# Scores as three half-height products per head, even and odd heads on the two halves of TensorE's rows

## The chip, the core and the metric

The kernel runs on one core of a Trainium2 chip. Its engines work side by side, each through its own list of instructions in the order of the program: TensorE (PE: matrix products; PEld: the loads of its stationary operand), VectorE (DVE), ScalarE (ACT), GpSimd (POOL) and SyncE (SP, which issues most of the DMAs). TensorE writes to PSUM, which has eight banks of 2 KB in each of 128 partitions. The metric is the device time of one launch in microseconds; less is better.

## What is computed

Three blocks follow each other. Attention with a window of 128 positions for 4 sequences of 576 tokens and 8 heads of 64; a mixture of 4 experts (512 to 1024 to 512, weighted by given probabilities); and a soft mixture of 8 experts with 4 slots each. The change touches the first alone:

```python
B, H, S, D = q.shape                  # 4, 8, 576, 64
scores = scale * np.matmul(q, k.transpose(0, 1, 3, 2))
bias = slopes[:, None, None] * (-np.abs(rel).astype(np.float32))[None, :, :]
mask = (rel >= 0) & (rel < window)    # window 128
scores = np.where(mask, scores + bias[None], -1000000000.0)
attn = np.exp(scores - np.max(scores, axis=-1, keepdims=True))
attn = attn / (np.sum(attn, axis=-1, keepdims=True) + 1e-09)
out = np.matmul(attn, v)
```

## The kernel before, in words

The 2304 tokens are 18 tiles of 128. A tile needs the keys of itself and of the tile before it, two key blocks (one for the first tile of a launch or of a sequence that begins on a tile's edge). Numbers in float32 are split into a high and a low float16 part, so that a product of two of them is three float16 products: high by high, high by low, low by high.

**Scores.** `sp_qk_hi` and `sp_qk_lo` (lines 336 to 343) split q and k of a tile; for each head the 64 high columns stand beside the 64 low ones. `tr_q` and `tr_k` turn this over (a DMA transpose, TensorE for the first two tiles), so that a head has its high part in rows 0 to 63 and its low part in rows 64 to 127. One product over 128 rows then gives high by high plus low by low (line 393). For the mixed terms `swap_q` (lines 375 to 378) makes a second copy of q with the halves exchanged, two copies on VectorE, and line 398 adds the second product. A head and a key block take 2 products of 128 by 128 by 128. Line 396 adds the mask of tiles in which a sequence ends. `qk` does this for two heads (a head pair), whose scores lie in one PSUM bank; tags S0 and S1, one bank each, take turns from pair to pair.

**Softmax and values.** `soft` adds the bias and takes the maximum (line 409, VectorE), the exponential (414) and the float16 parts (419 on ScalarE, 420 on GpSimd), then transposes them. `pv` (line 440) multiplies with v into one of two banks, X0 or X1, for four heads each; `xn` normalises (lines 449 to 451).

**Order.** `att_step` emits one step per tile and head pair, 72 in all; products with v trail by up to three steps. The first mixture's products are emitted between the steps: lines 300 and 310 in float32 for tiles 0 and 1, 242 and 261 for tiles 2 to 7 with expert 0, then units of 256 hidden columns (first layer: 742, later 727 from seven sums; second layer: 829). Line 193, with 192, splits the weights. A scheduler that works with its own timeline then sets each engine's final order; the text's order is not the program's. TensorE takes its list strictly in that order. From tile 8 on, the first layer holds the bank X1 too (its tile C).

Of the kernel before, what the change touches and what calls it, by code (L numbers as in the profile page):

```python
# [20 lines left out]
def kernel(  # L21
# [47 lines left out]
    def nm(s):  # L69
        uid[0] += 1  # L70
        return f"{s}_{uid[0]}"
# [262 lines left out]
            raw[nme, i] = t  # L334

    def sp_qk_hi(nme, i):
        t = at([P, H, 2, D], F16, nme + "s", 1)
        nc.scalar.activation(out=t[:, :, 0], in_=raw[nme, i], func=AF.Copy)
        (qqs if nme == "q" else kks)[i] = t

    def sp_qk_lo(nme, i, eng):
        t = (qqs if nme == "q" else kks)[i]
        return eng.tensor_tensor(out=t[:, :, 1], in0=raw[nme, i], in1=t[:, :, 0], op=ALU.subtract).ins

    def sp_v_hi(i):
        vvs[i] = vbuf[i % 4]
# [16 lines left out]
        nc.scalar.activation(out=dst[:, hb:nb], in_=pt[:, hb:nb], func=AF.Copy)  # L363

    def tr_k(i, pe=False):
        t = at([P, H, P], F16, "kT", 3)
        trans(t, kks[i].rearrange("p h a d -> p (h a d)"), H, pe)
        kT[i] = t

    def tr_q(i, pe=False):  # L370
        t = at([P, 2, H, P], F16, "qT", 2)
        trans(t[:, 0], qqs[i].rearrange("p h a d -> p (h a d)"), H, pe)
        qT[i] = t

    def swap_q(i):
        t = qT[i]
        nc.vector.tensor_copy(t[0:D, 1], t[D:P, 0])
        nc.vector.tensor_copy(t[D:P, 1], t[0:D, 0])  # L378

    def kbs(i):  # L380
        return [1] if i in first else [0, 1]

    fixes = {(0, 0): P, (0, 1): P // 2, (1, 0): P // 2}

    def qk(i, hp):
        st = ps.tile([P, 2, 2 * P], F32, tag=f"S{hp % 2}", name=nm("s"), bufs=1)
        fix = 0 if i in split else (1 if (i - 1) in split else None)
        for hl in range(2):
            h = 2 * hp + hl
            for kb in kbs(i):  # L390
                o = st[:, hl, kb * P:(kb + 1) * P]
                mv = kT[i - 1 + kb][:, h]
                nc.tensor.matmul(o, lhsT=qT[i][:, 0, h], rhs=mv, start=True, stop=False)  # L393
                fx = fixes.get((fix, kb))
                if fx:
                    nc.tensor.matmul(o[:, 0:fx], lhsT=(fixa if fix == 0 else ones1), rhs=negs[:, 0:fx],
                                     start=False, stop=False)
                nc.tensor.matmul(o, lhsT=qT[i][:, 1, h], rhs=mv, start=False, stop=True)  # L398
        return st

    def soft(i, hp, st):
        kb0 = kbs(i)[0]
        if hp == 0:
            nmx[i] = at([P, H], F32, "nmx")
        c0, w = kb0 * P, (2 - kb0) * P
        et = at([P, 2, 2 * P], F32, "e", 3)
        for hl in range(2):
            h = 2 * hp + hl
            mx = nc.vector.tensor_tensor_reduce(out=et[:, hl, c0:], in0=st[:, hl, c0:], in1=bias[:, h, c0:],  # L409
                                                op0=ALU.add, op1=ALU.min, scale=-0.125, scalar=3.0e38,  # L410
                                                accum_out=nmx[i][:, h:h + 1])
        for hl in range(2):
            h = 2 * hp + hl
            nc.scalar.activation(out=et[:, hl, c0:], in_=et[:, hl, c0:], func=AF.Exp, scale=-1.0,  # L414
                                 bias=nmx[i][:, h:h + 1])
        e2 = at([P, 2, 2, 2 * P], F16, "e2", 3)
        if kb0:
            e2 = e2.rearrange("p a b c -> p (a b c)")[:, 0:4 * P].rearrange("p (a b c) -> p a b c", a=2, b=2)
        nc.scalar.activation(out=e2[:, :, 0], in_=et[:, :, c0:], func=AF.Copy)  # L419
        nc.gpsimd.tensor_tensor(out=e2[:, :, 1], in0=et[:, :, c0:], in1=e2[:, :, 0], op=ALU.subtract)  # L420
        nb = 4 * w // P
        eTt = at([P, 8, P], F16, "eT", 5)
        trans(eTt[:, 0:nb], e2.rearrange("p a b c -> p (a b c)"), nb, i < 2)
        eT[i, hp] = eTt
        return mx.ins

    def pv(i, hp):
        if hp % 2 == 0:
            xps[i, hp // 2] = ps1.tile([P, 512], F32, tag="X0" if i >= SG[1][0] + SG[1][1] else f"X{hp // 2}", name=nm("x"))[:, 0:4 * (D + 1)].rearrange(
                "p (h d) -> p h d", h=4)  # L430
        nk = len(kbs(i))
        kb0 = kbs(i)[0]
        t = eT.pop((i, hp))
        for hl in range(2):
            h = 2 * hp + hl
            o = xps[i, hp // 2][:, h % 4]
            for kb in kbs(i):
                for ea, va in ((0, 0), (0, 1), (1, 0)):
                    w = D + 1 - va
                    nc.tensor.matmul(o[:, 0:w], lhsT=t[:, (hl * 2 + ea) * nk + kb - kb0],  # L440
                                     rhs=vvs[i - 1 + kb][:, h, va, 0:w],
                                     start=(kb == kb0 and ea == 0 and va == 0), stop=(kb == 1 and ea == 1))
# [68 lines left out]
        build_bias(scr, range(6, H))  # L511
    tr_q(0, True)
    tr_k(0, True)
    swap_q(0)
    sp_v_hi(0)
    sp_v_lo(0)
    LAG = 3
# [37 lines left out]
    def att_step(n, work=None):  # L555
# [18 lines left out]
        if n < NS:  # L574
            if hp < 3 and i + 2 < NT:
                ld(i + 2, "qkv"[hp])
            if i + 1 < NT:
# [6 lines left out]
                    sp_qk_lo("k", i + 1, nc.gpsimd)  # L584
                elif hp == 2:
                    tr_k(i + 1, i + 1 < PE_T)
                    swap_q(i + 1)
                    sp_v_hi(i + 1)
                else:
                    sp_v_lo(i + 1)  # L590
# [723 lines left out]
```

## Time and profile before

| what | us |
|---|---|
| three timed runs | 931.27, 931.63, 937.0 |
| their median | 931.63 |
| the profiled execution: its own time | 936.76 |
| its span, first to last instruction | 935.0 |

The profile is of one execution, 5.1 us above the median of the three. Busy time is the time in which an engine had an instruction under way. TensorE's products are pipelined: the length of one says how long it takes from start to (modelled) end, and the next may start long before that, so the pace is read from the distance of starts. A timeline row that says x6 is six instructions in one row.

### The profile page before, as it was taken

What the parts mean: (1) busy time and instruction counts of PE and PEld (TensorE: products, weight loads), DVE (VectorE), ACT (ScalarE), POOL (GpSimd) and SP (SyncE); (2) the same over time, 40 slices, a digit from 0 to 9 for tenths busy, and PEclk for the clock granted to TensorE, in tenths of its full rate; (3) what the DMA queues carried; (4) which work ended last, traced back from release to release, by engine and by line L of the source; (5) the groups of instructions that cost most, each with busy time, mean ns of one, the idle gap of its engine ahead of it and who ended that gap; (6) DMA issues with size and microseconds to landing.
All of it is one profiled execution on the core that took longest, in us unless ns stands there. A gap on an engine that the chain in (4) does not pass through costs nothing.

```text
span 935.0 us, 16158 instructions
## 1 busy us (share of the span) xinstructions
PE 885.7 (95%) x6302; PEld 509.6 (55%) x6302; DVE 535.4 (57%) x1225; ACT 389.4 (42%) x806; POOL 183.4 (20%) x177
## 2 busy tenths in 40 slices
PE   5779799899999999999999999999999899999797
PEld 3747567554544454545555555555556566666432
DVE  5965755535645445548866775687554465445422
ACT  5965555534634343434445443445232233222222
POOL 4544454400221221300102010150021100000000
PEclk9889899999999999999999999999999999999799
DMA  9699998937785564344545645497674855437896
GB/s 262 118 184 199 207 208 145 166 56 199 186 172 132 143 136 113 68 107 141 126 141 152 180 125 159 142 344 226 181 167 163 185 208 192 161 132 252 303 377 233
DMA packets 252813, 165.80 MB, mean 177 GB/s; under 512 B 191120, under 2 KB 221872, under 8 KB 252736
## 3 DMA queue, kind: packets, MB, share of 16 engines
q1 hardware_dynamic: 249616, 153.65, 62.9%
q0 software_dynamic: 3120, 11.11, 4.0%
q8 instruction: 49, 0.80, 0.3%
q14 instruction: 28, 0.23, 0.1%
HBM read 104.44 MB, written 27.79 MB: 141 GB/s over the span
## 4 chain that ended last, share of the span: by engine, by line
PE 75%; DVE 6%; DMA 6%; issue 6%; ACT 2%; POOL 1%; SPq 0%; ACTq 0%; POOLq 0%; DVEq 0%
PE l L829 31%; PE l L742 12%; PE A L727 9%; PE C L727 4%; PE l L242 2%; DMA xtb<-xsb 2%; PE B L727 2%; DVE w L193 2%; PE hp L1246 2%; PE x L440 2%; PE so_ps L1264 2%; PE l L261 2%; PE l2f L310 1%; PE fp L1277 1%; DMA XA<-xs 1%
## 5 line engine op out<-in xcount | busy, mean ns | idle before, releaser
L829 PE MATMUL l<-w,HA 128*128 128x512 f16 x1536 | 366.5, 381 | 0.3 <-DVE acc L271 0.3
L829 PEld LDWEIGHTS <-HA 128*128 128x128 f16 x1536 | 148.1, 98 | 157.6 <-issue 5.0
L727 PEld LDWEIGHTS <-w 128*128 128x128 f16 x1344 | 129.8, 98 | 69.6 <-DMA w<-dw 3.3
L420 POOL TENSOR_TENSOR e<-e,e 128x512 f16<-128x512 f32 (+1 forms) x72 | 82.6, 1152 | 339.4 <-ACT e L419 205.3
L742 PE MATMUL l<-XA,w 128*128 128x512 f16 x576 | 131.7, 379 | 0.0
L271 DVE SCALAR_TENSOR_TENSOR acc<-l,pr,acc 128x512 f32<-128x512 f32 x118 | 88.0, 747 | 50.7 <-PE l L829 49.8
L742 PEld LDWEIGHTS <-w 128*128 128x128 f16 x576 | 55.4, 98 | 64.6
L768 ACT ACTIVATE HA<-XA 128x384 f16<-128x384 f32 (+1 forms) x96 | 44.8, 467 | 107.0 <-DVE XA L779 106.9
L414 ACT ACTIVATE e<-e,nmx 128x256 f32<-128x256 f32 (+1 forms) x144 | 64.0, 487 | 57.5 <-DVE nmx L409 57.4
L775 ACT ACTIVATE XA<-A 128x384 f32<-128x384 f32 (+1 forms) x96 | 41.3, 431 | 75.9 <-PE A L727 75.4
L746 DVE SCALAR_TENSOR_TENSOR HA<-l,HA 128x512 f16<-128x512 f32 x48 | 33.1, 689 | 58.9 <-ACT HA L745 58.8
L409 DVE CUSTOM_DVE_ANT_0 e<-s,bias 128x256 f32<-128x256 f32 (+1 forms) x144 | 52.5, 403 | 24.9 <-PE s L398 23.6
L727 PE MATMUL C<-SA,w 128*128 128x384 f16 (+1 forms) x384 | 63.4, 299 | 0.0
L745 ACT ACTIVATE HA<-l 128x512 f16<-128x512 f32 x48 | 28.4, 591 | 84.1 <-PE l L742 84.0
L769 DVE SCALAR_TENSOR_TENSOR HA<-XA,HA 128x384 f16<-128x384 f32 (+1 forms) x96 | 48.4, 504 | 25.7 <-ACT HA L768 25.3
L727 PE MATMUL A<-SA,w 128*128 128x384 f16 (+1 forms) x384 | 63.1, 299 | 0.0
L393 PE MATMUL s<-kT,qT 128*128 128x128 f16 x272 | 44.2, 229 | 7.3 <-DVE nmx L409 5.0
L779 DVE TENSOR_TENSOR XA<-XA,C 128x384 f32<-128x384 f32 (+1 forms) x64 | 30.8, 481 | 32.8 <-ACT XA L775 27.5
L193 DVE SCALAR_TENSOR_TENSOR w<-SA,w 128x512 f16<-128x512 f32 x54 | 39.1, 758 | 15.6 <-ACT w L192 15.5
L398 PE MATMUL s<-kT,qT 128*128 128x128 f16 x272 | 43.6, 230 | 2.8 <-DVE qT L378 2.8
L440 PE MATMUL x<-vv,eT 128*128 128x65 f16 (+1 forms) x816 | 41.3, 197 | 4.0 <-DVE eT L362 3.0
L419 ACT ACTIVATE e<-e 128x512 f16<-128x512 f32 (+1 forms) x72 | 43.0, 599 | 1.4 <-DMA eT<-e 0.3
(221 smaller groups left out, 1124.1 us busy)
## 6 DMA issues: line engine op xcount, KB each, us to landing
dw<-w SPq DMA_DIRECT2D x16, 896.0 KB, 4.9
w<-dw SPq DMA_DIRECT2D x28, 512.0 KB, 4.7
w<-dw SPq DMA_DIRECT2D x16, 896.0 KB, 4.6
m<-in_moe_w_dram SPq DMA_DIRECT2D x24, 512.0 KB, 6.7
SA<-in_moe_w_dram SPq DMA_DIRECT2D x18, 512.0 KB, 4.7
dw<-w SPq DMA_DIRECT2D x16, 512.0 KB, 3.5
stg<-in_moe_w_dram SPq DMA_DIRECT2D x32, 256.0 KB, 3.4
m<-in_moe_w_dram POOLq DMA_DIRECT2D x13, 512.0 KB, 6.7
```

What stands on the lines that cost most here:

```text
L193: nc.vector.scalar_tensor_tensor(out=dst[:, 1, a:b], in0=src[:, a:b], scalar=WS, in1=dst[:, 0, a:b], op0=ALU.mult, op1=ALU.subtract)
L271: nc.vector.scalar_tensor_tensor(out=a, in0=pt, scalar=p, in1=a, op0=ALU.mult, op1=ALU.add)
L393: nc.tensor.matmul(o, lhsT=qT[i][:, 0, h], rhs=mv, start=True, stop=False)
L409: mx = nc.vector.tensor_tensor_reduce(out=et[:, hl, c0:], in0=st[:, hl, c0:], in1=bias[:, h, c0:], op0=ALU.add, op1=ALU.min, scale=-0.125, ...
L414: nc.scalar.activation(out=et[:, hl, c0:], in_=et[:, hl, c0:], func=AF.Exp, scale=-1.0, bias=nmx[i][:, h:h + 1])
L420: nc.gpsimd.tensor_tensor(out=e2[:, :, 1], in0=et[:, :, c0:], in1=e2[:, :, 0], op=ALU.subtract)
L440: nc.tensor.matmul(o[:, 0:w], lhsT=t[:, (hl * 2 + ea) * nk + kb - kb0], rhs=vvs[i - 1 + kb][:, h, va, 0:w], start=(kb == kb0 and ea == 0 a ...
L727: nc.tensor.matmul(o, lhsT=wq_[:, blk, wa, kc], rhs=xf(xa, kc), start=(first and kc == 0 and wa == 0 and xa == 0), stop=(kc == 1 and wa == 1),
L742: nc.tensor.matmul(pt, lhsT=w[:, wa, o:o + P], rhs=x_ap(4 * c, 512, xa, kc), start=(kc == 0 and wa == 0 and xa == 0), stop=(kc == KC - 1 a ...
L768: nc.scalar.activation(out=o[:, 0], in_=src, func=AF.Relu)
L769: nc.vector.scalar_tensor_tensor(out=o[:, 1], in0=src, scalar=0.0, in1=o[:, 0], op0=ALU.max, op1=ALU.subtract)
L829: nc.tensor.matmul(pt, lhsT=us[y]["hap"](z, ha, t - SG[sg][0]), rhs=W2[e, qds[y]][:, wa, z * 512:(z + 1) * 512], start=(y == 0 and z == 0 ...
```

## The change

The halves move. `sp_qk_hi` and `sp_qk_lo` now store all heads' high parts and then all low parts, [part, head, 64]. A transposed block of 128 rows is then one part of two heads: the even head in rows 0 to 63, the odd one in rows 64 to 127. `qk` makes the three products of each head (`qa`, `ka` say which parts) over 64 rows, for the even and the odd head in turn. The swapped copy of q and low by low are gone. Each head writes to a bank of its own; up to tile 13 three banks take turns (S0, S1, X1), after it S0 and S1. `pv` has X0 alone.

```diff
--- before.py
+++ after.py
@@ -334,13 +334,13 @@
             raw[nme, i] = t
 
     def sp_qk_hi(nme, i):
-        t = at([P, H, 2, D], F16, nme + "s", 1)
-        nc.scalar.activation(out=t[:, :, 0], in_=raw[nme, i], func=AF.Copy)
+        t = at([P, 2, H, D], F16, nme + "s", 1)
+        nc.scalar.activation(out=t[:, 0], in_=raw[nme, i], func=AF.Copy)
         (qqs if nme == "q" else kks)[i] = t
 
     def sp_qk_lo(nme, i, eng):
         t = (qqs if nme == "q" else kks)[i]
-        return eng.tensor_tensor(out=t[:, :, 1], in0=raw[nme, i], in1=t[:, :, 0], op=ALU.subtract).ins
+        return eng.tensor_tensor(out=t[:, 1], in0=raw[nme, i], in1=t[:, 0], op=ALU.subtract).ins
 
     def sp_v_hi(i):
         vvs[i] = vbuf[i % 4]
@@ -363,39 +363,41 @@
         nc.scalar.activation(out=dst[:, hb:nb], in_=pt[:, hb:nb], func=AF.Copy)
 
     def tr_k(i, pe=False):
-        t = at([P, H, P], F16, "kT", 3)
-        trans(t, kks[i].rearrange("p h a d -> p (h a d)"), H, pe)
-        kT[i] = t
+        t = kT[i] = at([P, 2, H // 2, P], F16, "kT", 3)
+        trans(t.rearrange("p a h t -> p (a h) t"), kks[i].rearrange("p a h d -> p (a h d)"), H, pe)
 
     def tr_q(i, pe=False):
-        t = at([P, 2, H, P], F16, "qT", 2)
-        trans(t[:, 0], qqs[i].rearrange("p h a d -> p (h a d)"), H, pe)
-        qT[i] = t
-
-    def swap_q(i):
-        t = qT[i]
-        nc.vector.tensor_copy(t[0:D, 1], t[D:P, 0])
-        nc.vector.tensor_copy(t[D:P, 1], t[0:D, 0])
+        t = qT[i] = at([P, 2, H // 2, P], F16, "qT", 2)
+        trans(t.rearrange("p a h t -> p (a h) t"), qqs[i].rearrange("p a h d -> p (a h d)"), H, pe)
 
     def kbs(i):
         return [1] if i in first else [0, 1]
 
     fixes = {(0, 0): P, (0, 1): P // 2, (1, 0): P // 2}
 
+    banks = [0]
+
     def qk(i, hp):
-        st = ps.tile([P, 2, 2 * P], F32, tag=f"S{hp % 2}", name=nm("s"), bufs=1)
+
+        st = []
+        for _ in range(2):
+            tg = banks[0] % (3 if i < SG[2][0] else 2)
+            banks[0] += 1
+            st.append(ps.tile([P, 512], F32, tag=f"S{tg}", name=nm("s"), bufs=1) if tg < 2 else
+                      ps1.tile([P, 512], F32, tag="X1", name=nm("s")))
         fix = 0 if i in split else (1 if (i - 1) in split else None)
-        for hl in range(2):
-            h = 2 * hp + hl
-            for kb in kbs(i):
-                o = st[:, hl, kb * P:(kb + 1) * P]
-                mv = kT[i - 1 + kb][:, h]
-                nc.tensor.matmul(o, lhsT=qT[i][:, 0, h], rhs=mv, start=True, stop=False)
-                fx = fixes.get((fix, kb))
-                if fx:
-                    nc.tensor.matmul(o[:, 0:fx], lhsT=(fixa if fix == 0 else ones1), rhs=negs[:, 0:fx],
-                                     start=False, stop=False)
-                nc.tensor.matmul(o, lhsT=qT[i][:, 1, h], rhs=mv, start=False, stop=True)
+        for kb in kbs(i):
+            kt = kT[i - 1 + kb]
+            fx = fixes.get((fix, kb))
+            for qa, ka in ((0, 0), (0, 1), (1, 0)):
+                for hl in range(2):
+                    d = slice(hl * D, hl * D + D)
+                    nc.tensor.matmul(st[hl][:, kb * P:(kb + 1) * P], lhsT=qT[i][d, qa, hp], rhs=kt[d, ka, hp],
+                                     start=(qa + ka == 0), stop=(qa == 1))
+                if fx and qa + ka == 0:
+                    for s_ in st:
+                        nc.tensor.matmul(s_[:, kb * P:kb * P + fx], lhsT=(fixa if fix == 0 else ones1),
+                                         rhs=negs[:, 0:fx], start=False, stop=False)
         return st
 
     def soft(i, hp, st):
@@ -406,7 +408,7 @@
         et = at([P, 2, 2 * P], F32, "e", 3)
         for hl in range(2):
             h = 2 * hp + hl
-            mx = nc.vector.tensor_tensor_reduce(out=et[:, hl, c0:], in0=st[:, hl, c0:], in1=bias[:, h, c0:],
+            mx = nc.vector.tensor_tensor_reduce(out=et[:, hl, c0:], in0=st[hl][:, c0:2 * P], in1=bias[:, h, c0:],
                                                 op0=ALU.add, op1=ALU.min, scale=-0.125, scalar=3.0e38,
                                                 accum_out=nmx[i][:, h:h + 1])
         for hl in range(2):
@@ -426,7 +428,7 @@
 
     def pv(i, hp):
         if hp % 2 == 0:
-            xps[i, hp // 2] = ps1.tile([P, 512], F32, tag="X0" if i >= SG[1][0] + SG[1][1] else f"X{hp // 2}", name=nm("x"))[:, 0:4 * (D + 1)].rearrange(
+            xps[i, hp // 2] = ps1.tile([P, 512], F32, tag="X0", name=nm("x"))[:, 0:4 * (D + 1)].rearrange(
                 "p (h d) -> p h d", h=4)
         nk = len(kbs(i))
         kb0 = kbs(i)[0]
@@ -511,7 +513,6 @@
         build_bias(scr, range(6, H))
     tr_q(0, True)
     tr_k(0, True)
-    swap_q(0)
     sp_v_hi(0)
     sp_v_lo(0)
     LAG = 3
@@ -584,7 +585,6 @@
                     sp_qk_lo("k", i + 1, nc.gpsimd)
                 elif hp == 2:
                     tr_k(i + 1, i + 1 < PE_T)
-                    swap_q(i + 1)
                     sp_v_hi(i + 1)
                 else:
                     sp_v_lo(i + 1)
```

The built programs differ in TensorE's list as follows. Near the list's start, the scores of tile 0, before; `s_188` and `s_222` are the banks of its first two head pairs:

```order
L398 LDWEIGHTS qT_160
L398 MATMUL s_188<-kT_172,qT_160 128x128
L393 LDWEIGHTS qT_160
L393 MATMUL s_188<-kT_172,qT_160 128x128
L398 LDWEIGHTS qT_160
L398 MATMUL s_188<-kT_172,qT_160 128x128
L398 LDWEIGHTS qT_160
L398 MATMUL s_222<-kT_172,qT_160 128x128
L393 LDWEIGHTS qT_160
L393 MATMUL s_222<-kT_172,qT_160 128x128
L398 LDWEIGHTS qT_160
L398 MATMUL s_222<-kT_172,qT_160 128x128
```

All products are over 128 rows. The same place after the change, where `s_186` and `s_187` are the even and the odd head of the first pair, `s_223` and `s_224` those of the second:

```order
L395 LDWEIGHTS qT_160
L395 MATMUL s_187<-kT_172,qT_160 128x128
L395 LDWEIGHTS qT_160
L395 MATMUL s_223<-kT_172,qT_160 128x128
L395 LDWEIGHTS qT_160
L395 MATMUL s_223<-kT_172,qT_160 128x128
L395 LDWEIGHTS qT_160
L395 MATMUL s_224<-kT_172,qT_160 128x128
L395 LDWEIGHTS qT_160
L395 MATMUL s_224<-kT_172,qT_160 128x128
L395 LDWEIGHTS qT_160
L395 MATMUL s_224<-kT_172,qT_160 128x128
```

Even and odd are not in turn here: two of `s_223` follow each other, then three of `s_224`; the scheduler has moved single products.

The last head pair of the attention, among the second layer of the mixture, before:

```order
L398 LDWEIGHTS qT_5593
L398 MATMUL s_6347<-kT_5713,qT_5593 128x128
L393 LDWEIGHTS qT_5593
L393 MATMUL s_6347<-kT_5088,qT_5593 128x128
L398 LDWEIGHTS qT_5593
L398 MATMUL s_6347<-kT_5088,qT_5593 128x128
L393 LDWEIGHTS qT_5593
L393 MATMUL s_6347<-kT_5713,qT_5593 128x128
L398 LDWEIGHTS qT_5593
L398 MATMUL s_6347<-kT_5713,qT_5593 128x128
L440 LDWEIGHTS eT_5971
L440 MATMUL x_6374<-vv_6_126,eT_5971 128x65
```

From line 398 to line 440 nothing changes in height. After the change, the end of the last pair (`s_6650` even, `s_6651` odd):

```order
L395 LDWEIGHTS qT_5873
L395 MATMUL s_6651<-kT_5998,qT_5873 128x128
L395 LDWEIGHTS qT_5873
L395 MATMUL s_6650<-kT_5998,qT_5873 128x128
L829 LDWEIGHTS HA
L829 MATMUL l_901_6605<-w_6467,HA 128x512
L829 LDWEIGHTS HA
L829 MATMUL l_901_6605<-w_6467,HA 128x512
L395 LDWEIGHTS qT_5873
L395 MATMUL s_6651<-kT_5998,qT_5873 128x128
L442 LDWEIGHTS eT_6264
L442 MATMUL x_6682<-vv_6_126,eT_6264 128x65
```

Two products of line 829 over 128 rows now stand between the last two scores over 64 rows.

Counted over the whole lists: before, 544 score products (lines 393 and 398) of 128 rows; after, 816 of 64 rows (line 395), in 130 unbroken runs between other work. In the runs 294 times a product of one half is followed by one of the other half, pairs counted once; the other 228 stand alone. Before the first product of line 829 stand 224 of the 544, and after the change 330 of the 816, in 59 runs, with 77 pairs and 176 alone; behind it 320 before, and 486 after, in 71 runs, with 217 pairs and 52 alone. Each run is one passage into the height of 64 and one out of it. The number of mask products (48) and all others stays.

## Rows read from the trace of the kernel before

**Rows 1.** The page, parts 1 and 2: busy time; TensorE and its clock in 40 slices.

```profile
PE 885.7 (95%) x6302; PEld 509.6 (55%) x6302; DVE 535.4 (57%) x1225; ACT 389.4 (42%) x806; POOL 183.4 (20%) x177
PE   5779799899999999999999999999999899999797
PEclk9889899999999999999999999999999999999799
```

**Rows 2.** Line 829 by itself: duration min/median/max, first and last start, forms.

```profile
L829 PE MATMUL l<-w,HA x1536: 376/379/634, 137.9 to 867.3; 128*128 128x512 f16 x192
```

**Rows 3.** Windows of three stages: length; busy PE, PEld, DVE, ACT, POOL; clock, DMA, GB/s.

```profile
0.00:138.00 138.00, 109.09 (x1073) 81.72 (x1074) 92.10 (x275) 84.24 (x183) 66.11 (x68) 0.90 0.95 196
138.00:200.00 62.00, 59.19 (x546) 40.63 (x545) 30.87 (x100) 31.83 (x71) 26.19 (x24) 1.00 0.84 143
200.00:600.00 400.00, 400.00 (x2500) 206.59 (x2498) 243.96 (x519) 167.02 (x313) 59.84 (x51) 1.00 0.54 140
```

**Rows 4.** Chain of waits by line: 0 to 138, 138 to 200, 200 to 600 us.

```profile
by line: DVE w L193 10.8%; PE l2f L310 9.7%; DVE e L409 6.0%; PE l1f L300 5.9%; issue 5.3%; DMA XA<-xs 4.1%; PE l L242 3.6%; DMA kT<-ks 3.3%; DMA SA<-in_moe_w_dram 3.0%; PE l L261 2.8%; DVE qT L377 2.8%; ACT w L192 2.4%; DVE qT L378 2.2%; D
...
by line: PE l L242 27.7%; PE l L829 13.6%; PE l L261 13.5%; issue 6.0%; DMA qT<-qs 5.3%; DMA kT<-ks 5.2%; PE x L440 4.9%; SPq L356 3.9%; PE s L398 2.7%; PE s L393 2.7%; ACT e L419 2.0%; ACT e L414 2.0%; POOL xs L478 1.8%; ACT HA L745 1.6%; 
...
by line: PE l L829 40.3%; PE l L742 28.5%; issue 9.8%; PE A L727 8.0%; PE C L727 3.9%; PE x L440 2.6%; PE B L727 2.0%; PE s L393 1.6%; PE s L398 1.6%; DMA XA<-xs 1.4%; PE l L261 0.6%; POOL xs L478 0.3%; POOL e L420 0.3%; PE s L396 0.2%; POO
```

**Rows 5.** Timeline of TensorE at 305 us: start, length, instruction.

```profile
305.02 0.22 PE L393 MATMUL s<-kT,qT 128*128 128x128 f16 x1
305.07 0.22 PE L398 MATMUL s<-kT,qT 128*128 128x128 f16 x1
...
305.41 0.22 PE L398 MATMUL s<-kT,qT 128*128 128x128 f16 x1
305.47 0.53 PE L440 MATMUL x<-vv,eT 128*128 128x65 f16 x12
```

**Rows 6.** Costliest groups of the page: a weight load, the two score products.

```profile
L829 PEld LDWEIGHTS <-HA 128*128 128x128 f16 x1536 | 148.1, 98 | 157.6 <-issue 5.0
...
L393 PE MATMUL s<-kT,qT 128*128 128x128 f16 x272 | 44.2, 229 | 7.3 <-DVE nmx L409 5.0
...
L398 PE MATMUL s<-kT,qT 128*128 128x128 f16 x272 | 43.6, 230 | 2.8 <-DVE qT L378 2.8
```

**Rows 7.** Timeline of TensorE at 764 us, around a transpose of 32 rows.

```profile
764.31 0.82 PE L727 MATMUL A<-XA,w 128*128 128x256 f16 x6
765.06 0.43 PE L1102 MATMUL lt<-ident,dtb 32*128 32x32 f32 x4
765.42 0.83 PE L727 MATMUL A<-XA,w 128*128 128x256 f16 x6
766.09 0.82 PE L727 MATMUL C<-SA,w 128*128 128x256 f16 x6
766.74 0.59 PE L829 MATMUL l<-w,HA 128*128 128x512 f16 x2
```

**Rows 8.** Timeline of TensorE at 773 us, around products of 32 output columns.

```profile
773.46 1.24 PE L829 MATMUL l<-w,HA 128*128 128x512 f16 x5
774.63 1.07 PE L1129 MATMUL sp<-acc,dd 128*32 128x512 f32 x8
775.63 0.61 PE L727 MATMUL A<-XA,w 128*128 128x256 f16 x4
```

**Rows 9.** Line 1129 by itself: duration min/median/max, forms.

```profile
L1129 PE MATMUL sp<-acc,dd x32: 592/605/617, 726.2 to 788.5; 128*32 128x512 f32 x32
```

**Rows 10.** Windows of the two swap copies alone (lines 377, then 378), 0 to 138 us.

```profile
0.00:138.00 138.00, 7.49 (x9) 0.90 0.95 196
...
0.00:138.00 138.00, 7.24 (x9) 0.90 0.95 196
```

**Rows 11.** Waits of TensorE, 0 to 138 us: total, times, longest.

```profile
PE s L393 <- DVE nmx L409: 5.0, 5, 1.5
...
PE s L398 <- DVE qT L378: 2.8, 3, 1.8
```

## The prediction

> **What bounds the kernel now.** I began with the page's parts 1 and 2 [rows 1]. TensorE is busy for 885.7 of 935.0 us; in the 40 slices nearly all gaps of its row lie in the first eight and the last few, and its granted clock drops below full only there. So there are two regimes, and the change has work in both. The border is where the second layer begins, at 137.9 us [rows 2]. The windows show the two: up to 138 us TensorE is busy for 109 us, VectorE for 92, ScalarE for 84, the DMA share is 0.95 and the mean clock 0.90; from 200 to 600 us TensorE is busy for all of 400 us at clock 1.00 [rows 3]. The chain of waits says the same by line. Up to 138 us the lines of VectorE, DMA and ScalarE are mixed with 22% of TensorE (9.7, 5.9, 3.6 and 2.8), and the two swap copies are 2.8 and 2.2%, that is 6.9 us; from 138 to 200 us TensorE's six lines make 65%; from 200 on nearly all is TensorE [rows 4]. What is added to TensorE's list is paid in full behind 200 us and in part before.
>
> **Columns.** At 305 us a run of eight score products starts every 55.7 ns (0.39 us over seven steps), with weight loads of 98 ns hidden beside them [rows 5, 6]. The 544 products of now [rows 6] are 544 such steps. Of the 816 new ones, 588 stand in 294 pairs of unlike halves; if a pair takes one step, the list has 294 + 228 = 522 steps, 22 fewer, 1.2 us. The design would have 408; the scheduler's order has taken the rest away. By stage: before line 829, 77 + 176 = 253 steps in place of 224, +29 or +1.6 us; behind it 217 + 52 = 269 in place of 320, -51 or -2.8 us.
>
> Does a pair take one step? No product of 64 rows is in this trace. The nearest rows are the products on 32 columns at 773 us: eight, each some 605 ns long, take 1.07 us together, so that four run side by side [rows 8, 9]. For rows I take that over. The other end is a step for each half: 816 steps. And twelve products of 65 columns take 0.53 us, one about 0.2 us long, so some 30 ns a step including its weight load [rows 5]; two halves need no more than 60 ns for issue, near one step.
>
> **Changing height.** This is the term that decides. At 764 us six products of 256 columns come every 0.108 us (766.09 to 766.74), so after 764.31 the next was due at 764.96; the transpose over 32 rows starts at 765.06, 0.10 us late. Its four steps take 0.43 us with 0.22 for the last, so the last starts at 765.27; full products go on at 765.42, 0.15 later in place of some 0.07 [rows 7]. At 773 us five products at 0.215 us end in a start due at 774.54, and the products on 32 columns start at 774.63 [rows 8]. Each change of the array's shape costs about 0.09 us, in and out, with no wait shown. The new list has 130 runs of 64 rows, 260 changes, 23.4 us in all: before line 829 118 changes or 10.6 us, behind it 142 or 12.8 us. The bounds for 64 rows: nothing (the shape is another) and the whole pipeline, 0.22 us, the length of one score product [rows 5]. I take 0.09, the value of both shapes that the trace has.
>
> The Trainium skill (TensorEngine Tiling (Array Packing), Key Properties) says that changing the tiling mode drains TensorE. The trace agrees in kind, but the measured 0.09 us is less than the 0.27 us that a product of 256 columns lasts beyond its 0.11 us of pace would suggest: a full drain would be about 0.16 us a change, and the 142 late changes alone would then cost 23 us. The measurement decides.
>
> **Stage behind 138 us.** 12.8 - 2.8 = +10.0 us. In 138 to 200 us a third of the chain is not TensorE; I take 1 us off: +9.0.
>
> **Stage up to 138 us.** TensorE's list grows by 10.6 + 1.6 = 12.2 us; its part of the chain is 22% in the listed lines, I use a quarter: +3.1. The swap copies go: 7.49 + 7.24 us of VectorE [rows 10], of which 6.9 us lie on the chain. What is late next there is ScalarE, busy for 84 us against VectorE's 92 [rows 3], and the DMAs; I take 4 us as gained, with 0 and 14.7 as ends. TensorE's waits for the second copy (2.8 us in three) go with it [rows 11] and are in these 4.
>
> Banks: until now a pair's bank is asked for again after two pairs, then after one and a half; and the values have one bank in place of two. TensorE waits 5.0 us in five for the maximum that frees a bank [rows 11]; 5.0 x 2 / 1.5 is 1.7 us more, and with the values' bank I take +2.5, between 0 and 8 (a microsecond for each of the eight tiles of this stage). What is queued behind such a wait on TensorE is the first layer of the mixture, whose results ScalarE and VectorE wait for. Behind 138 us a bank's next user stands several us of products later in the list, so I take no wait. The transposes, splits and the mask products are the same in number and size: nothing.
>
> **Sum.** 9.0 + 3.1 - 4 + 2.5 = +10.6 us. Against the profiled execution that is 936.8 + 10.6 = 947.4; that execution is 5.1 us above the median, and against the median it is 931.6 + 10.6 = 942.2 us.
>
> **Rivals.**
> (a) Not slower, by VectorE. In the first 138 us the split of weights and the maximum (lines 193 and 409) are VectorE's largest parts of the chain. If all 14.7 us of the copies come off it and not 4, the sum falls by 10.7 to -0.1: 931.5 us. For it: VectorE leads the chain there. Against: ScalarE and DMA are nearly as full. It decides once the first product of line 829 starts some 9 us earlier than 138, which pays for the whole later stage.
> (b) Changes to 64 rows cost nothing. Then -2.8 behind, 1.6 / 4 = +0.4 before, -4 and +2.5: -3.9, 927.7 us. Against: both shapes in the trace pay.
> (c) The change doesn't do what it says: the halves run one after the other. Then 816 steps: behind line 829 166 x 55.7 ns = +9.2 in place of -2.8, before it 106 x 55.7 ns / 4 = +1.5 in place of +0.4: 13.1 more, 955.3 us. Against: the columns of 32 run side by side.
> (d) Weight loads for the same half are not hidden. The 52 late and 176 early single steps would pay 98 ns each: 5.1 + 17.2 / 4 = 9.4 more, 951.6 us. Against: the four transposes over the same 32 rows come 0.07 us apart [rows 7], less than a load. The Trainium skill (TensorE: Matmul & The Clock Gate, The mechanism) lets a load overlap a running product only in other rows; here loads of 128 rows hide beside products of 128 rows, so the trace speaks against it.
> (e) The values' single bank holds TensorE up: 8 us in place of 2.5 and a longer early stage at the lower clock: 949 us.
>
> **How the numbers follow.** Forecast 0.48, its own range 935 to 949; (a) 0.20, (b) 0.10, (c) 0.13, (d) 0.04, (e) 0.05. A measurement of this kernel can tell about 1% from no change, 9.3 us: the borders are 922.3 and 940.9. Slower by more: 0.6 of the forecast (0.29), nearly all of (c), (d) and (e) (0.22): 0.51. Faster by more: a fifth of (b) and a tenth of (a), 0.04, called 0.05. The rest, 0.44, is within 1%. The range reaches from 929, below (a) and above (b), to 956, just above (c).
>
> **What would show it.** In the new profile: a gap of about 0.09 us beyond the pace at each change between 64 and 128 rows, and none inside runs; in runs that alternate, starts in pairs a few ns apart every 56 ns (a start every 56 ns would be (c)); the stretch from the first product of line 829 to the end about 9 us longer; that first product within 4 us of 138; VectorE busy some 15 us less up to that product, with no lines 377 and 378. I am wrong if the later stage isn't longer, or if the early one moves by more than 8 us either way.

## The result and the profile after

The changed kernel takes 945.56 us (median of four runs, 943.72 to 948.77); the kernel before, on the same chip, 933.06 (four runs, 931.27 to 937.0). The ratio is 1.0132, with an interval from 1.0083 to 1.018: slower by 12.3 us, between 7.7 and 16.8. The forecast was 942.2 and 10.6 us. The profiled execution of the changed kernel, 943.7 us, is the fastest of its four, and that of the kernel before was 3.7 us above its median, so the two traces lie only 7 us apart; what a stage gained or lost is read from them with that in mind.

The page after, parts 1 and 2 (engines, TensorE and its clock in 40 slices), against [rows 1]:

```profile
PE 906.7 (96%) x6574; PEld 503.0 (53%) x6574; DVE 509.2 (54%) x1189; ACT 390.0 (41%) x806; POOL 179.0 (19%) x177
PE   5898999999999999999999999999999899999797
PEclk9996999999999999999999999999999999999799
```

TensorE is busy for 21 us more, VectorE for 26 us less. Of the first eight slices five were below 9, now three are.

The first product of line 829, against [rows 2]:

```profile
L829 PE MATMUL l<-w,HA x1536: 376/379/391, 140.8 to 873.1; 128*128 128x512 f16 x192
```

It starts at 140.8 us in place of 137.9. The windows of the stages, against [rows 3]:

```profile
0.00:138.00 138.00, 119.34 (x1149) 80.99 (x1150) 72.25 (x247) 85.38 (x182) 63.90 (x69) 0.91 0.97 197
138.00:200.00 62.00, 62.00 (x597) 40.34 (x594) 25.64 (x94) 29.96 (x67) 22.47 (x22) 1.00 0.75 135
200.00:600.00 400.00, 400.00 (x2585) 196.84 (x2584) 236.88 (x504) 165.96 (x313) 59.60 (x51) 1.00 0.53 137
```

Up to 138 us TensorE is busy for 119.3 us in place of 109.1, so its idle time there has shrunk by a third, from 28.9 to 18.7 us; VectorE has fallen from 92 to 72. Who leads the chain there has changed. Its lines up to 138 us, against the first of [rows 4]:

```profile
by line: PE l2f L310 10.4%; PE l L742 7.7%; PE l L242 7.1%; PE l L261 6.9%; PE s L395 6.4%; PE l1f L300 5.4%; DMA eT<-e 5.0%; PE x L442 4.4%; DMA kT<-ks 3.8%; DMA XA<-xs 3.7%; DMA SA<-in_moe_w_dram 3.4%; PE tp L360 1.3%; ACT e L416 1.0%; AC
```

Six lines of TensorE and the transposes' DMA are ahead; lines 193 and 409 (now 411), the first and third of before, are no longer among the lines shown. TensorE's lines shown make 50% here; before they made 22%, as much as VectorE's four. The stage is TensorE's now.

The scores themselves. The groups of the page, against [rows 6]:

```profile
L395 PE MATMUL s<-kT,qT 64*128 64x128 f16 x816 | 57.8, 234 | 4.9 <-DVE nmx L411 3.8
...
L395 PEld LDWEIGHTS <-qT 64*128 64x128 f16 x816 | 32.9, 99 | 32.6 <-issue 27.2
```

Runs from the timeline of TensorE, against [rows 5]: one of nine, two that by the list hold one half alone (245.25 the even one, 246.23 the odd one), and one in turn. The timeline does not say which half a product is of; that is read from the list:

```profile
153.66 0.51 PE L395 MATMUL s<-kT,qT 64*128 64x128 f16 x9
...
244.29 1.03 PE L742 MATMUL l<-XA,w 128*128 128x512 f16 x4
245.25 0.51 PE L395 MATMUL s<-kT,qT 64*128 64x128 f16 x6
245.69 0.60 PE L829 MATMUL l<-w,HA 128*128 128x512 f16 x2
246.23 0.51 PE L395 MATMUL s<-kT,qT 64*128 64x128 f16 x6
...
299.79 0.51 PE L395 MATMUL s<-kT,qT 64*128 64x128 f16 x12
```

Twelve products in turn take 0.51 us from the first start to the last end, six of one half alone take 0.51 us too: two unlike halves share a step of 56 ns, 0.22 being the length of the last. Six evens followed by three odds, the run at 153.66, also take 0.51. The change of height is there as forecast: at 244.29 four products of 512 columns at 0.216 us end in a start due at 245.15; the scores start at 245.25. The last of these six starts at 245.54 (245.25 + 0.51 - 0.22 of length), and line 829 goes on at 245.69, 0.15 later in place of 0.056. Each way costs about 0.10. By the starts of the single products, all 55 runs behind 200 us pay it: 0.09 to 0.10 us beyond the pace on the way in and again on the way out.

### The profile page after: what moved, and what is told of

It is laid out like the page before. It is cut to its first block, busy times and chain, and to the rows that moved or that the text cites. A ratio compares the mean times of both kernels' runs of the same rounds, so it can differ in the third digit from the quotient of the medians.

```text
span 941.9 us, 16678 instructions
## 1 busy us (share of the span) xinstructions
PE 906.7 (96%) x6574; PEld 503.0 (53%) x6574; DVE 509.2 (54%) x1189; ACT 390.0 (41%) x806; POOL 179.0 (19%) x177
## 4 chain that ended last, share of the span: by engine, by line
PE 85%; DMA 6%; DVE 2%; ACT 1%; issue 0%; SPq 0%; POOL 0%; ACTq 0%; POOLq 0%; DVEq 0%
PE l L829 32%; PE l L742 13%; PE A L727 10%; PE C L727 5%; PE s L395 3%; PE l L242 3%; PE l L261 3%; PE x L442 3%; DMA w<-dw 3%; PE B L727 2%; PE hp L1246 2%; DMA xtb<-xsb 2%; PE so_ps L1264 2%; PE l2f L310 2%; PE fp L1277 1%; PE l1f L300 1%
## 5 line engine op out<-in xcount | busy, mean ns | idle before, releaser
L829 PE MATMUL l<-w,HA 128*128 128x512 f16 x1536 | 362.6, 379 | 0.2 <-DVE acc L271 0.2
L422 POOL TENSOR_TENSOR e<-e,e 128x512 f16<-128x512 f32 (+1 forms) x72 | 80.6, 1122 | 331.3 <-ACT e L421 207.4
L411 DVE CUSTOM_DVE_ANT_0 e<-s,bias 128x256 f32<-128x256 f32 (+1 forms) x144 | 54.4, 405 | 33.0 <-PE s L395 26.5
L769 DVE SCALAR_TENSOR_TENSOR HA<-XA,HA 128x384 f16<-128x384 f32 (+1 forms) x96 | 51.1, 533 | 25.8 <-ACT HA L768 25.3
L395 PE MATMUL s<-kT,qT 64*128 64x128 f16 x816 | 57.8, 234 | 4.9 <-DVE nmx L411 3.8
L193 DVE SCALAR_TENSOR_TENSOR w<-SA,w 128x512 f16<-128x512 f32 x54 | 39.5, 770 | 21.4 <-ACT w L192 21.4
L395 PEld LDWEIGHTS <-qT 64*128 64x128 f16 x816 | 32.9, 99 | 32.6 <-issue 27.2
L442 PE MATMUL x<-vv,eT 128*128 128x65 f16 (+1 forms) x816 | 43.2, 199 | 3.6 <-DVE x L453 1.6
```

The costliest lines, as they stand in the source:

```text
L395: nc.tensor.matmul(st[hl][:, kb * P:(kb + 1) * P], lhsT=qT[i][d, qa, hp], rhs=kt[d, ka, hp], start=(qa + ka == 0), stop=(qa == 1))
L769: nc.vector.scalar_tensor_tensor(out=o[:, 1], in0=src, scalar=0.0, in1=o[:, 0], op0=ALU.max, op1=ALU.subtract)
L829: nc.tensor.matmul(pt, lhsT=us[y]["hap"](z, ha, t - SG[sg][0]), rhs=W2[e, qds[y]][:, wa, z * 512:(z + 1) * 512], start=(y == 0 and z == 0 ...
```

## The experiments

In all of them a time is a ratio to runs of the kernel before on the same chip, with a 95% interval, and is turned into microseconds with 933.

**Changes of height alone.** The kernel before, with 72 products of zeros added to the scores, over 64 rows or over 128:

```diff
                 nc.tensor.matmul(o, lhsT=qT[i][:, 0, h], rhs=mv, start=True, stop=False)
...
+                if hl == 0 and kb == 1:
+                    nc.tensor.matmul(o, lhsT=zz[0:D], rhs=zz[0:D], start=False, stop=False)
                 nc.tensor.matmul(o, lhsT=qT[i][:, 1, h], rhs=mv, start=False, stop=True)
```

In the second kernel `zz[0:D]` is `zz`.

> The kernel before, with one more product per head pair: zeros over 64 rows, added into the scores of the even head, so that TensorE changes height twice per pair. Its list has 72 such single runs, 30 ahead of the first product of line 829 and 42 behind it. If each change costs 0.09 us and is paid behind line 829 in full (theory): 42 x (2 x 0.092 + 0.056) = +10.1 us there, and a quarter of 30 x 0.24 = 7.2 ahead, +1.8: 12 us more than before, 9 to 13. If changing to 64 rows costs nothing and the time comes from banks and order (rival): the products alone, 42 x 0.056 + 0.4 = +2.8 us.

Measured: 950.61 us, ratio 1.0192 (1.0145 to 1.0239), +17.9 us: more than either theory; the next kernel says how much of it is not the height.

> The same 72 added products of zeros, but over all 128 rows, so that no height changes. Both theories: 72 steps of 0.056 us, 2.4 us behind line 829 and under 1 ahead, so +2 to +3.5 us against before. The difference to the kernel with 64 rows is the price of the changes alone: theory 84 changes x 0.092 = 7.7 us behind line 829 and up to 1.5 ahead, rival 0.

Measured: 938.9 us, ratio 1.0073 (1.0036 to 1.0109), +6.8 us, above both theories. 72 full steps are 4.0 us, so moving the list around may be worth some 3 us by itself, which the interval (3.4 to 10.2) does not tell from nothing. The difference between the two, 1.2% or 11 us for 144 changes, is what the height costs: 0.077 us for each. The two intervals leave some 5.5 us either way, so 0.04 to 0.11. The timeline of the first of the two shows the price at one place (lines 395 and 402 are the two score products, 401 the zeros):

```profile
299.89 0.22 PE L402 MATMUL s<-kT,qT 128*128 128x128 f16 x1
299.95 0.22 PE L395 MATMUL s<-kT,qT 128*128 128x128 f16 x1
300.10 0.23 PE L401 MATMUL s<-zz 64*128 64x128 f16 x1
300.26 0.23 PE L402 MATMUL s<-kT,qT 128*128 128x128 f16 x1
300.32 0.22 PE L395 MATMUL s<-kT,qT 128*128 128x128 f16 x1
```

0.06 us from a full product to the next, but 0.15 to the one over 64 rows and 0.16 back: 0.09 to 0.10 each way. 144 x 0.092 would be 13.2 us, and with the forecast's quarter for the first stage it would be 9.2; the times cannot tell these apart. In the two traces, with spans of 947.2 and 940.8 us, line 829 (833 here) starts thus with changes and without:

```profile
L833 PE MATMUL l<-w,HA x1536: 376/379/631, 138.7 to 877.6; 128*128 128x512 f16 x192
```

```profile
L833 PE MATMUL l<-w,HA x1536: 377/379/634, 137.9 to 870.9; 128*128 128x512 f16 x192
```

That is 0.8 us ahead of it for 60 changes and 5.6 behind it for 84. In this pair the changes in the first stage cost little.

**The copies alone.** The kernel before without `swap_q`; line 398 reads the unswapped half.

```diff
-                nc.tensor.matmul(o, lhsT=qT[i][:, 1, h], rhs=mv, start=False, stop=True)
+                nc.tensor.matmul(o, lhsT=qT[i][:, 0, h], rhs=mv, start=False, stop=True)
...
-    swap_q(0)
...
-                    swap_q(i + 1)
```

> The kernel before without the two swap copies; line 398 reads the unswapped half, so the mixed terms high by low and low by high are left out of the scores. All else, 128 rows and the banks too, stays. Forecast: 4 us faster (0 to 7), all of it ahead of line 829. Rival (a): the whole of VectorE's 14.7 us comes off, 12 to 15 us faster. A third reading: something else sets that stage, and nothing changes (within 1.5 us).

Measured: 926.31 us, ratio 0.9937 (0.9912 to 0.9962), 5.9 us faster (3.5 to 8.2). Within the forecast's 0 to 7, nearer its upper end; rival (a) with 12 to 15 is out. The trace has it ahead of line 829, whose first product starts at 132.2 us in place of 137.9.

**The banks alone.** The kernel before with the changed kernel's allocation of PSUM:

```diff
-        st = ps.tile([P, 2, 2 * P], F32, tag=f"S{hp % 2}", name=nm("s"), bufs=1)
+        st = []
+        for _ in range(2):
+            tg = banks[0] % (3 if i < SG[2][0] else 2)
+            banks[0] += 1
+            st.append(ps.tile([P, 512], F32, tag=f"S{tg}", name=nm("s"), bufs=1) if tg < 2 else
+                      ps1.tile([P, 512], F32, tag="X1", name=nm("s")))
...
-            xps[i, hp // 2] = ps1.tile([P, 512], F32, tag="X0" if i >= SG[1][0] + SG[1][1] else f"X{hp // 2}", name=nm("x"))[:, 0:4 * (D + 1)].rearrange(
+            xps[i, hp // 2] = ps1.tile([P, 512], F32, tag="X0", name=nm("x"))[:, 0:4 * (D + 1)].rearrange(
```

> The kernel before with the banks of the change alone: a bank for each head, three in turn up to tile 13 and two behind, and one bank for the values; products over 128 rows and the swap copies stay. Theory: +2.5 us (0 to 8), ahead of line 829. Rival, that banks and the order that follows from them make the change slower: +9 us or more, and behind line 829 too.

Measured: 927.55 us, ratio 0.9949 (0.9922 to 0.9976), 4.8 us faster (2.2 to 7.3). Neither theory: I expected a loss, and both the forecast's +2.5 and rival (e) are out. It computes everything and is faster than both kernels. Its windows up to 200 us and from there to 600, and behind them the first of the kernel before:

```profile
0.00:200.00 200.00, 166.10 (x1616) 118.75 (x1617) 115.96 (x371) 113.80 (x250) 89.31 (x91) 0.97 0.94 179
200.00:600.00 400.00, 400.00 (x2512) 207.03 (x2511) 244.62 (x523) 169.88 (x319) 60.19 (x52) 1.00 0.55 141
```

```profile
0.00:200.00 200.00, 168.28 (x1617) 122.36 (x1618) 122.97 (x375) 116.07 (x253) 92.30 (x92) 0.93 0.92 180
```

In the first 200 us TensorE is busy for 166.1 us against the 168.3 of the kernel before, at a mean clock of 0.97 against 0.93; I did not test whether the clock is the cause or goes with it. And the wait that the forecast took to grow, TensorE's for the maximum that frees a bank, shrinks: in the first 200 us it is 2.2 us in five, where the kernel before has 5.0 in five [rows 11].

```profile
PE s L400 <- DVE nmx L416: 2.2, 5, 0.8
```

**Both.** The same with the copies left out (and the mixed terms with them).

> The kernel before with the banks of the change and without the swap copies; line 398 reads the unswapped half (the mixed terms are left out). Singly the banks gave 5.6 us and the copies 6.9. If both shorten different waits: 921, 10 us or more faster than before. If they shorten the same stretch of the first stage, so that the second gives nothing more, as the dead copies in the changed kernel suggest: 925 to 929.

Measured: 925.13 us, ratio 0.9906 (0.988 to 0.9933), 8.8 us faster. The two singly make 10.7. The time lies at the edge of the second reading (925 to 929), but the interval, 6.3 to 11.2 us, holds a full sum as well: most of both shows together, and whether all of it would cannot be told.

**The copies put back** into the changed kernel as dead work:

```diff
+    def swap_q(i):
+        t = qT[i].rearrange("p a h t -> p (a h) t")
+        z = at([P, H, P], F16, "zT", 1)
+        nc.vector.tensor_copy(z[0:D], t[D:P])
+        nc.vector.tensor_copy(z[D:P], t[0:D])
```

> The changed kernel with the two swap copies put back as dead work on VectorE, into a tile that nobody reads. If they cost here what their removal gave to the kernel before: 4 to 8 us slower than the changed kernel, all of it ahead of line 829. If the stage is set by TensorE by now: within 2 us of the changed kernel.

Measured: 946.22 us, ratio 1.014 (1.0111 to 1.0168), 0.7 us beside the changed kernel's 1.0132. So no cost shows, though the two intervals leave some 5 us either way. The traces agree: the first product of line 829 starts at 141.1 us, in the changed kernel at 140.8. This tests VectorE's time alone, since nothing waits for the dead copies; in the kernel before, line 398 waited for them (2.8 us [rows 11]).

**Runs in one piece, as units of the scheduler.** `qk` in a section that is scheduled as a whole, masks over 64 rows, halves in turn, halves apart, or four heads together:

```diff
+        with tc.tile_critical():
...
+                    for qa, ka in ((0, 0), (0, 1), (1, 0)):
+                        for hl in range(2):
+                            d = slice(hl * D, hl * D + D)
+                            nc.tensor.matmul(bk[hl][:, j, kb * P:(kb + 1) * P], lhsT=qT[i][d, qa, hp + j],
+                                             rhs=kt[d, ka, hp + j], start=(qa + ka == 0), stop=(qa == 1))
```

> The changed kernel with each head pair's products handed to the scheduler as one unit, even and odd in turn, and the mask products over 64 rows too: 66 runs in place of 130, 432 steps in place of 522 (and 48 mask steps). From the parts measured so far, against the kernel before: 132 changes x 0.092 = +12.1 us, (432 - 592) x 0.056 = -8.9, swap copies -5.9, banks -4.8: -7.5, 925 us, between 920 and 931. Rival: the time is in the order that the scheduler is free to make, and a unit that waits for both banks holds TensorE up: no faster than the changed kernel, 943 or more.

Measured: 1045.88 us, ratio 1.1191 (1.1155 to 1.1226).

> The same units, but in each key block the three products of the even head first and then the three of the odd one, so that halves seldom meet: 658 steps in place of 432, the same 66 runs. If unlike halves share a step (theory): +226 x 0.056 = +12.6 us against the units in turn, of which 7.6 lie behind line 829: 8 to 13 us slower than they. If halves run one after the other whatever the order (rival c): within 2 us of them.

Measured: 1047.72 us, ratio 1.1208 (1.1161 to 1.1255).

> Units of four heads: the even heads of two pairs share one bank, the odd ones another, and both pairs' products stand in one run, 35 runs in place of 66, 432 steps. Theory: 62 changes fewer, 62 x 0.092 = 5.7 us faster than units of a pair, 3 to 6. Rival: banks held for four heads make TensorE wait ahead of line 829, which takes that back: no faster than units of a pair.

Measured: 1022.27 us, ratio 1.0946 (1.0914 to 1.0978). The waits of TensorE in the first of these:

```profile
PE s L402 <- issue: 20.6, 34, 2.3
PE s L402 <- DMA raw<-in_q_dram: 20.4, 2, 17.6
PE s L402 <- ACT e L425: 8.7, 6, 2.2
PE s L402 <- DMA SA<-in_moe_w_dram: 6.1, 2, 3.7
...
PE s L402 <- DVE w L193: 3.4, 1, 3.4
```

A unit waits for loads, splits of weights and exponentials that its products don't read (line 402 holds the score products here). So as a test of the total the three failed: the section brought over 100 us in two of them, and 88 in the third, of waits of its own, in line with the rival's sign but for another reason. Their runs can be read all the same. A run of 12 in turn, from the first kernel, and one of 12 as three even, three odd, twice, from the second:

```profile
502.95 0.51 PE L402 MATMUL s<-kT,qT 64*128 64x128 f16 x12 [0.44 <-ACT w L711]
```

```profile
537.35 0.52 PE L402 MATMUL s<-kT,qT 64*128 64x128 f16 x12 [1.77 <-issue]
```

0.51 and 0.52 us. In strict order, with a step shared only where unlike halves meet, halves apart would need nine steps, 8 x 0.056 + 0.22 = 0.67 us; six are what the longer half needs. Like the run of nine above, this says that each half goes through its own products, and that their order within these runs did not matter. My count of 522 steps was too high by 14: run by run the longer half makes 508.

**Runs in one piece by priority.** Score products with priority in the scheduler, pinned to their order, masks over 64 rows; one head pair, then two, in a run:

```diff
+        with tc.high_priority():
...
+                        if len(mms) > 1:
+                            tc.keep_in_program_order(mms[-1])
```

> The changed kernel with the score products given priority in the scheduler and pinned to their order, and the mask products over 64 rows: 73 runs in place of 130, 433 steps (the longer half of each run) in place of 508 and 48 mask steps; no unit, so no wait but that for the banks and the operands. Theory, each change 0.092 us and halves sharing steps: against the changed kernel 114 changes fewer, -10.5 us, and 123 steps, -6.9: up to 17 us, 928 if all of it shows, 935 if 60% does; against the kernel before between 8 faster and 3 slower. Rival: the slowness came with the order and banks, not with changes: 943 or more.

Measured: 942.11 us, ratio 1.0087 (1.0051 to 1.0122): 4.2 us less than the changed kernel, of the 17 that the list is shorter; the two intervals leave some 5.5 us either way, so a gain is not shown, and 17 are out.

> The same with four heads in a run, two even heads in one bank and two odd ones in another: 37 runs, 432 steps. Theory: 72 changes fewer than with one pair, 6.6 us, so 4 to 7 us faster than that kernel and faster than the one before. Rival: a bank held for two heads makes TensorE and VectorE wait ahead of line 829, which costs more than 6 us: no faster than with one pair.

Measured: 944.53 us, ratio 1.0121 (1.0089 to 1.0154); the rival's answer. Windows up to 200 us and on to 600, of the changed kernel, with a pair in a run, and with four heads:

```profile
0.00:200.00 200.00, 181.34 (x1740) 121.34 (x1741) 97.89 (x341) 115.34 (x248) 86.37 (x90) 0.94 0.90 178
200.00:600.00 400.00, 400.00 (x2585) 196.84 (x2584) 236.88 (x504) 165.96 (x313) 59.60 (x51) 1.00 0.53 137
```

```profile
0.00:200.00 200.00, 169.72 (x1800) 116.46 (x1801) 104.67 (x368) 122.60 (x267) 94.28 (x96) 0.94 0.95 185
200.00:600.00 400.00, 396.10 (x2534) 198.10 (x2533) 228.43 (x480) 155.29 (x295) 51.48 (x45) 1.00 0.53 135
```

```profile
0.00:200.00 200.00, 160.51 (x1782) 114.46 (x1783) 101.77 (x365) 120.94 (x265) 92.18 (x96) 0.93 0.98 186
200.00:600.00 400.00, 396.92 (x2546) 200.41 (x2545) 227.31 (x481) 155.84 (x296) 51.63 (x45) 1.00 0.51 134
```

TensorE's list is shorter, but it idles more: 18.7 us in the first 200 after the change, 30.3 with a pair in a run, 39.5 with four heads, and 3.9 and 3.1 us more between 200 and 600, where the changed kernel has none. (The traced execution with a pair, 945.45 us, is 3.3 above its median.) What the whole runs save by the count, 10.5 us in changes and 6.9 in steps, mostly comes back as waiting. TensorE's longest wait in the first 200 us with a pair is the one for the maximum that frees a bank, but the changed kernel has most of it too; with four heads the longest is for a DMA:

```profile
PE s L397 <- DVE nmx L417: 5.1, 5, 2.3
```

```profile
PE s L395 <- DVE nmx L411: 3.8, 3, 3.4
```

```profile
PE l L242 <- DMA XA<-xs: 13.8, 3, 8.0
```

So this wait is 1.3 of the 11.6 us that the pair adds there, and the rest is spread over many lines. That the scheduler had broken the runs up to fill such waits is my reading; no run shows it by itself.

**The copies on GpSimd**, with the banks, to see if the 4 us between them and the kernel without copies are to be had:

```diff
-        nc.vector.tensor_copy(t[0:D, 1], t[D:P, 0])
-        nc.vector.tensor_copy(t[D:P, 1], t[0:D, 0])
+        nc.gpsimd.tensor_copy(t[0:D, 1], t[D:P, 0])
+        nc.gpsimd.tensor_copy(t[D:P, 1], t[0:D, 0])
```

> The kernel before with the banks of the change, and with the two swap copies on GpSimd in place of VectorE; products over 128 rows, all terms there. GpSimd is busy for 66 of the first 138 us against VectorE's 92. If what the copies cost is VectorE's time: near the kernel with the banks and no copies, 925 to 927, faster than both kernels. If GpSimd's copies are long or come late to line 398: 928 to 935, no better than the banks alone.

Measured: 936.7 us, ratio 1.0032 (1.0007 to 1.0057). They are not, and the time lies above both readings: the banks' gain is gone as well. A copy is longer on GpSimd than it was on VectorE (the kernel before, second line):

```profile
L377 POOL COPY qT<-qT x18: 1032/1032/1385, 8.3 to 447.3; 64x1024 f16<-64x1024 f16 x18
...
L377 DVE COPY qT<-qT x18: 422/676/1344, 8.6 to 445.2; 64x1024 f16<-64x1024 f16 x18
```

TensorE waits for the copies only 1.5 us in the first 200, but for the maximum 7.7, against 2.2 with the banks alone. How the one leads to the other is not shown.

## Why the prediction was right, and where two of its terms were not

**Direction, size and cause** held: slower, 12.3 us for 10.6, through 260 changes of height. TensorE's busy time grew by 21.0 us. The new list by the measured prices is longer by 260 x 0.092 for the changes less 36 x 0.056 for the steps saved, 21.9, which is near, though a busy time also depends on the granted clock. The price of a change, 0.09 us from two other shapes, is 0.09 to 0.10 in the trace after and 0.077 net of cover in the pair of experiments. Rival (b) falls with it. Halves that share a step, taken over from products of 32 columns, hold; (c) falls. Runs of one half alone come 58 ns apart ((0.51 - 0.22) / 5) beside loads of 99 ns, so the loads are hidden and (d) falls. The sentence of the Trainium skill (TensorE: Matmul & The Clock Gate, The mechanism) that a load overlaps running products only where the rows differ does not hold for these runs, whose products and loads are all of the same 64 rows. The same section of the Trainium skill also has loads for a background weight buffer pulled ahead; whether that is at work here no run shows. That the sum came so near is in part luck: several of its terms were mis-sized, and against each other.

**"Stage up to 138 us": two terms were mis-sized, and their errors cancel.** I charged a quarter of what TensorE's list grows by there (+3.1 of 12.2), by TensorE's share of the old chain, and credited 4 us for the copies less 2.5 for the banks. The runs say: copies and banks together are worth 8.8 us, not 1.5, and the banks help where I expected waits. Against the kernel with those banks and no copies, the changed one is slower by 1.0132 / 0.9906, 2.3% or 21 us, some 5 either way; its list is longer by the 21.9 us above. So the new list is paid nearly in full: -8.8 + 21.9 = +13.1, and 12.3 were measured. The traces say the same for the first stage. Line 829 of the kernel with the banks and no copies (834 there; its span is 923.9 us) and its chain up to 138 us:

```profile
L834 PE MATMUL l<-w,HA x1536: 377/380/391, 130.9 to 855.2; 128*128 128x512 f16 x192
```

```profile
by line: DMA kT<-ks 10.1%; PE l L747 6.5%; DMA XA<-xs 6.3%; PE l1f L300 5.9%; PE l L242 4.7%; SPq L356 4.2%; ACT e L421 4.0%; ACT w L192 4.0%; DVE e L416 3.4%; issue 3.0%; DMA qT<-qs 2.9%; ACT e L426 2.8%; POOL e L427 2.7%; DMA eT<-e 2.4%; 
```

From there the first product of line 829 moves from 130.9 to 140.8 us, 9.9 us for a list that is longer by some 12 there, not 3.1. This is a balance of times: between these two kernels TensorE's busy time grows by 28.9 us (877.8 and 906.7), 7 more than the list, and its idle time falls by 10.9. What the 7 are is open. The step that failed is using the share of the old chain for a stage whose leader the change itself moves. It is not the missing copies that make TensorE lead: without them, and with the banks, its lines shown are 17% of this chain, and a DMA is first; with the changes of height on its list they are 50%. The dead copies, without a cost that shows in the changed kernel, fit this.

**"Stage behind 138 us"** (+9.0) is +4.0 in the traces. The sign that I named is the stretch from the first product of line 829 to the end; here it is with the stretch ahead of it, before and after:

```profile
0.00:137.90 137.90, 108.99 (x1072) 81.65 (x1073) 92.10 (x275) 84.14 (x183) 66.11 (x68) 0.90 0.95 196
137.90:935.00 797.10, 776.74 (x5231) 427.99 (x5229) 443.32 (x950) 305.27 (x625) 117.29 (x109) 0.99 0.63 174
```

```profile
0.00:140.80 140.80, 122.14 (x1191) 83.32 (x1192) 74.45 (x257) 87.08 (x186) 64.25 (x69) 0.92 0.97 197
140.80:941.90 801.10, 784.51 (x5386) 419.71 (x5383) 434.78 (x933) 302.92 (x622) 114.75 (x108) 0.99 0.61 172
```

Behind the border TensorE is busy for 7.8 us more and idle for 3.8 us less, 2.8 of them between 138 and 200 us, where I took off 1. Ahead of it TensorE is busy for 13.2 us more and idle for 10.3 us less. So against the kernel before, 14 of the 21 us that TensorE is busy for longer came out of time in which it had idled. Line 742, the plain first layer, gives the same; its row before and after (first and last start in the middle):

```profile
L742 PE MATMUL l<-XA,w x576: 377/379/380, 125.7 to 423.4; 128*128 128x512 f16 x192
```

```profile
L742 PE MATMUL l<-XA,w x576: 377/379/391, 123.3 to 430.4; 128*128 128x512 f16 x192
```

From its first product to its last it is 297.7 us before and 307.1 after, 9.4 us more, but it begins ahead of the border, by 12.2 us before and by 17.5 after: 5.3 of the 9.4 lie there, and 4.1 behind. The last product of line 829 comes 5.8 us later (867.3 and 873.1): behind the attention nothing is added.

The price of the list behind the border was not what failed. Against the kernel with the banks and no copies the stretch is 8.1 us longer (793.0 and 801.1). What I left out there is what banks and copies give: the kernel before needs 797.1, 4.1 us more, where I put nothing. All this is one trace of each kernel. Those before and after lie 7.0 us apart and the times 12.3, and in which stage the other 5 us lie is not known.

**Signs I had named:** the gap at each change, starts in pairs (in the run at 299.79, 3 or 4 ns apart, a pair every 56 ns), and line 829 within 4 us of 138 (140.8) came out. The longer stretch behind it came out at 4.0 us in place of about 9. VectorE's relief up to 138 us is 20 us, 15 were named.

**What stays open** is why the banks help. Ahead of line 829 the kernel with the banks and no copies has the same products as the kernel before, and its first stage is 7.0 us shorter:

```profile
0.00:130.90 130.90, 103.54 (x1073) 78.53 (x1074) 73.44 (x252) 85.07 (x185) 65.08 (x70) 0.93 1.01 209
```

5.5 us of that are TensorE's busy time (109.0 and 103.5), at a granted clock of 0.90 and 0.93, and only 1.5 its idle time. So in these two executions most of the gain is shorter busy time and not less waiting. Whether the clock is a cause, or the traced execution of the kernel before had little of it by chance, no run tests. Nor are the banks of the scores and the one bank for the values tested apart. The same banks with the copies on GpSimd give nothing, but the copies are longer there too.

## What to carry to other kernels

Count the places where the height of TensorE's products changes before counting the rows saved: here 22 steps' worth of saving by the forecast's count stood against 260 changes at 0.09 us, and whole runs are worth it only if TensorE does not then wait for the operands of a whole run. A scheduler that breaks runs up may be filling waits; here forcing it not to gave most of the time back as idle time. Where a change takes work off the engine that leads a stage and adds work to another, price the addition by the chain as it will be and not by its share of the old one: here 9.9 of some 12 us were paid, not a quarter. And where TensorE seems full, look for the idle time that is left, which takes up part of what is added: 3.8 us here behind 138 us.

## What I had not expected

Two halves keep their own order: products of unlike halves within a run overlap even when three of one half stand ahead of three of the other (twelve in 0.52 us, 0.51 in turn), so in these runs only the balance of the halves counted. The Trainium skill (TensorE: Matmul & The Clock Gate, The mechanism) has products start and end strictly in the list's order; these runs speak against that for unlike halves, and so against my own sentence in the section on the kernel before, that TensorE takes its list strictly in order. And an allocation of banks that looks tighter, one bank for the values in place of two, made the kernel before 4.8 us faster; that version, with products over 128 rows, is the fastest complete one found here (927.55 us, ratio 0.9949).
